# Local attention, token mixing and a gated MLP on one core: channel mixing and output by seven products of quarters, shorter angles, split value loads, constant matmuls, a new order

## The chip, the core and the metric

One core of one Trainium2 chip. The metric is the time of one execution in microseconds (us). TensorE (PE) multiplies matrices, VectorE (DVE), ScalarE (ACT) and GpSimd (POOL) do the elementwise work, SyncE (SP) issues all DMAs. SBUF has 128 partitions; PSUM has 8 banks of 128 x 512 f32, into which PE accumulates.

## What is computed

Two batches, 8 heads, 768 tokens, head width 64, model width 512. The reference, cut to what matters:

```python
# attention: window |i-j| < 16, and 24 summaries of blocks of 32 tokens
k_sum, v_sum = k.max over each block of 32, v.mean over each block of 32
scores = concat(where(window, q @ k.T / 8, -1e9), q @ k_sum.T / 8 + log(32))
a = softmax(scores);  x = a @ concat(v, v_sum)        # heads side by side: (2, 768, 512)
# token mixing by rotation
theta = x @ w_theta                                   # 512 x 512
y = w_tok_r @ (x * cos(theta)) + w_tok_i @ (x * sin(theta))   # 768 x 768 each
u = x + y
x = u + relu(u @ w_ch)                                # channel mixing, 512 x 512
# gated MLP
h = gelu_tanh(x @ w_in);  u, v = halves of h          # 512 x 1024
v = layernorm(v) * g_ln
v = w_sg @ v + b_sg                                   # 768 x 768 over tokens
out = x + (u * v) @ w_out                             # 512 x 512
```

The weights arrive as 64-bit floats; the kernel reads them as bits and puts f32 together itself.

## The kernel before

**Precision.** Every large product is made of three matmuls. Each f32 operand is split into a high part (a copy rounded to fp32r; L324 on ACT, L326 on POOL, L329 on DVE) and a low part (source minus high part, `diff`, L332, on DVE or POOL), and `mm3` (L337 to L339) adds high x high, high x low and low x high into one bank. "A product" below is such a triple.

**Weights.** `unit` (L406) loads 128 rows by one DMA of 512 KB (L414) and makes f32 by one ACT step (L420) and one DVE step (L427); then it splits.

**Attention** works on pairs of heads `p` (`at_pair`: loads of k, q, vT and vW; block maxima L472) and on half pairs `p_hf` (`at_unit`): scores `S` (mask L516, window L523, summaries L530), row maximum `m` (DVE L535), subtraction `d` (L541), exp `e` (ACT L549), transposes `PT` (L554) and their copies `Pt`, values `O` (L568), normalisation `n` (DVE L577, L578, L581), transposes `X` (L590) and copies and splits of x. Pairs 0 to 3 are batch 0; `n3_1` is the last normalisation of batch 0.

**Mixing.** `theta` (twelve row tiles `th0` to `th11`): four products, then on ACT the nearest whole number of turns `kk` (L615) and a correction `kb` (L618), on DVE two steps `ra` (L623) and `rr` (L629, a custom instruction) that bring the angle into reach of the sine; `rotated` makes |angle| (`ab`), cosine and sine on ACT (`sc`, L650, L651) and the products with x (L656). `mixed` adds the products `y` and then x (L693).

**Channel mixing** `ch` (in a batch: 4 output chunks x 2 token ranges of 512 and 256 x 4 products), relu and sum on DVE (L754). **MLP**: `in_v` (gelu L768, layernorm), `in_u` (gelu L799), `sg` (gate L815, product L820), `outp` (4 x 2 x 4 products, sum L833, DMA L836).

**Order.** Nothing schedules at run time. `PLAN`, a table of some 900 words such as `ch0_0_0_0.P.4` (step, engine, place), is played from first to last by `Steps.play` (L247); each engine gets its steps in that order and the places say which part of SBUF or which bank a result takes. A step waits for those it names and for whoever used its place. All DMAs lie on SP's queue in the table's order.

Of the kernel before, what the change touches and what calls it, by code (L numbers as in the profile page):

```python
# [9 lines left out]
F32 = mybir.dt.float32  # L10
# [24 lines left out]
C1 = 6.28125  # L35
C2 = 2.0 * math.pi - 6.28125
PI_LO = 3.1415925
# [6 lines left out]

PLAN = """
k1.S.2712 ones.V masks.G q0_0.S.2688 q1_0.S.168 warm.V.148 fill.P.0 k0.S.100 ks1.V.0 q2_1.S.76
identb.V S1_0.P.0.1 ks0.V.1 m1_0_1.V.2 m1_0_0.V.3 q0_1.S.52 S0_1.P.2.3 vT0.S.4 vT1.S.336 k2.S.288
d1_0_0.V.243 m0_1_1.V.4 m0_1_0.V.3 d1_0_1.V d0_1_0.V.198 d0_1_1.V ks2.V.3 e1_0.A q2_0.S.552
S0_0.P.4.5 m0_0_1.V.4 m0_0_0.V.2 d0_0_0.V.103 S2_0.P.3.2 S2_1.P.1.0 m2_0_0.V.1 d2_0_0.V.507
d0_0_1.V m2_0_1.V.1 d2_0_1.V m2_1_0.V.4 m2_1_1.V.1 e0_1.A e0_0.A e2_0.A vT3.S.459 q1_1.S.435  # L50
S1_1.P.4.6 PT1_0_1.P.5 sets.G m1_1_0.V.0 PT1_0_0.P.3 PT0_0_0.P.7 PT2_0_1.P.2 d2_1_0.V.243 d2_1_1.V
m1_1_1.V.4 d1_1_0.V.55 Pt0_0_0.A.435 d1_1_1.V vs0.G.5 v0_0.S.386 wth0d.S.704 wth0t.A.0 v0_1.S.655
sums.G v1_1.S.606 vp0.P.7 vm0.A.0 v1_0.S.911 vT2.S.863 PT0_0_1.P.1 vs3.G.6 e2_1.A k3.S.815
PT2_0_0.P.7 PT0_1_0.P.0 vs1.G.3 PT2_1_1.P.4 vs2.V.0 vp1.P.6 vr0_0.G wth2d.S.1088 Pt0_0_1.A.552
q3_1.S.582 wth1d.S.1024 q3_0.S.168 v2_0.S.975 e1_1.A vm1.A.1 wr0d.S.1280 v2_1.S.1231 v3_0.S.6
Pt1_0_0.A.124 O0_0_0.P.1 Pt1_0_1.A.100 v3_1.S.1182 wi0d.S.1472 vr0_1.G Pt2_0_1.V.1158 wth3d.S.1408
wri1d.S.1344 wri0d.S.1664 ks3.V.3 wi1d.S.1600 Pt0_1_0.A.435 O0_0_1.P n0_0.V.4.288 wth2t.A.1
PT0_1_1.P.6 vr1_0.G vp2.P.3 vp3.P.2 PT1_1_1.P.5 O1_0_0.P.0 vm3.V.0 PT1_1_0.P.1 wri2d.S.1536
Pt2_0_0.A.552 Pt2_1_1.A.124 Pt0_1_1.V.219 wth1t.A.2 PT2_1_0.P.7 wth0r.V.68 Pt1_1_1.A.195 O0_1_0.P.6
wth0h.G.2688 Pt2_1_0.A.435 k4.S.1872 wr1d.S.1808 O1_0_1.P vm2.V.2 n1_0.V.4 O0_1_1.P wth1r.V.256  # L60
vr2_0.A S3_0.P.3.4 n0_1.V.4.864 vr1_1.G Pt1_1_0.A.100 wth1h.A.1920 S3_1.P.7.0 m3_0_0.V.6 X0_0.P.1
m3_1_1.V.4 wr3d.S.1744 wth0l.G xe0_0.A O1_1_0.P.6 d3_0_0.V.770 X1_0.P.5 wth2r.V.68 m3_0_1.V.6
d3_0_1.V vr2_1.A vr3_0.A O2_0_0.P.1 wr0t.A.1 O2_1_0.P.3 O2_1_1.P xh0_0.G.2064 e3_0.A O1_1_1.P
O2_0_1.P xl0_0.G wr2d.S.2240 th1_0.P.4 m3_1_0.V.3 wr0r.V.224 xe1_0.A PT3_0_1.P.2 X0_1.P.5
wr0h.G.1984 n1_1.V.6 PT3_0_0.P.6 d3_1_0.V.103 xh1_0.A.528 d3_1_1.V xl1_0.G Pt3_0_1.A.195
Pt3_0_0.A.1158 e3_1.A wth1l.V wth2h.G.384 xe0_1.A n2_0.V.4 xh0_1.G.480 th0_0.P.2 wi0t.A.1 th2_0.P.6
vr3_1.A O3_0_0.P.0 O3_0_1.P PT3_1_1.P.1 xl0_1.G vT4.S.2192 X2_0.P.5 n2_1.V.3 q4_0.S.2168 xe2_0.A
PT3_1_0.P.3 th0_1.P X2_1.P.5 n3_0.V.4 Pt3_1_0.V.195 X3_0.P.3 wth2l.G wth3t.A.2 Pt3_1_1.V.1158
xh2_0.G.2064 O3_1_0.P.1 wth3r.V.256 O3_1_1.P xl2_0.G q4_1.S.2144 th3_0.P.0 xe3_0.V th1_1.P
wth3h.A.0 xh3_0.V.144 n3_1.V.4 th2_1.P ks4.V.3 X3_1.P.1 wth3l.G X1_1.P.3 xl3_0.G xe2_1.V th0_2.P  # L70
th0_3.P wri0t.A.2 xe1_1.V wi1t.A.0 th1_2.P wr0l.G xh1_1.A.528 th1_3.P q5_0.S.2120 xe3_1.V th2_2.P
xh3_1.V.96 xl1_1.V kk0.A.192 xh2_1.G.720 kb0.A.224 kk1.A.256 ra0.V.1440 kb1.A.192 v4_0.S.2447
th2_3.P rr0.V ab0_0.V.1408 S4_0.P.2.1 v4_1.S.2398 vs4.V.4 ra1.V.224 vp4.P.3 m4_0_0.V.6 m4_0_1.V.4
wi2d.S.2334 sc0_0.A vT5.S.2640 th4_0.P.4 th3_1.P xl2_1.G d4_0_0.V.2195 xl3_1.G th3_2.P th5_0.P.2
d4_0_1.V th3_3.P th4_1.P zm0_0.G v5_1.S.2591 q6_0.S.2310 vm4.A.0 vr4_0.A kk2.A.256 e4_0.A
wi0r.V.2559 zh0_0.A.464 k5.S.2511 rr1.V wri1t.A.1 PT4_0_0.P.1 wi0h.G.2048 q5_1.S.1128 PT4_0_1.P.3
ra2.V.1504 th4_2.P Pt4_0_0.A.2171 kk3.A.192 O4_0_0.P.1 wri0r.V.1472 wi0l.V zl0_0.G Pt4_0_1.V.2567
vr4_1.G wri0h.G.576 vs5.V.4 O4_0_1.P S4_1.P.3.6 ab1_0.A.2208 wr1t.A.2 vp5.P.5 th4_3.P sc1_0.A
ks5.V.6 n4_0.V.0.768 m4_1_0.V.4 wri0l.G wr1r.V.1408 y0_0_0_0.P.1.7 vm5.A.0 kk4.A.1472 v5_0.S.1079
# [181 lines left out]
def kernel(  # L261
# [648 lines left out]
```

## Time and profile before

| what | us |
|---|---|
| runs of the kernel before | 400.04, 401.49, 402.1 (median 401.49) |
| the profiled execution: its own time | 400.38 |
| its span (first to last instruction) | 398.6 |
| PE busy | 382.7 |
| DVE busy | 243.2 |
| POOL busy | 194.6 |
| ACT busy | 161.2 |

The profiled execution lies 1.1 us below the median, and 1.8 us lie around its span. [...] How long a matmul really holds PE is read from the distance of the starts.

### The profile page before, as it was taken

The page shows a single profiled execution, that of the slowest core. Times are in us where ns is not written, and L with a number is a line of the kernel's source. Part 1 is how long each engine was busy: PE and PEld are TensorE (multiplying, and loading weights), DVE is VectorE, ACT ScalarE, POOL GpSimd, SP SyncE. Part 2 cuts the span into 40 slices and gives each one's busy share as a digit, 9 for nine tenths or more (in the row PEclk, how much of TensorE's full clock was granted, in tenths as well). Part 3 has the DMA queues.
Part 4 walks back from the last instruction along what each step waited for, and adds up shares of the span by engine and source line. Part 5 has one row for each costly group of instructions (what it writes and reads, how often), then busy time and mean ns, then how long its engine had stood idle before and what let it go on. Part 6 is the DMA issues. An engine that isn't in the chain of part 4 may idle for free.

```text
span 398.6 us, 7716 instructions
## 1 busy us (share of the span) xinstructions
PE 382.7 (96%) x3104; PEld 328.3 (82%) x3104; DVE 243.2 (61%) x426; ACT 161.2 (40%) x291; POOL 194.6 (49%) x219
## 2 busy tenths in 40 slices
PE   7787999899999999999999999999999999999996
PEld 4666878688878888888888888888888888889885
DVE  4884899989989676526445836764571444117242
ACT  1385679879898663503321220414260020111000
POOL 6642678477642638317758454730620357417100
PEclk9695999989999999999999999999999999999999
DMA  7999994544164413204303000000011000000134
GB/s 266 303 330 353 346 250 134 157 124 129 37 228 159 132 54 135 104 0 152 140 0 107 1 2 0 0 2 1 2 53 39 2 0 2 0 2 0 41 119 158
DMA packets 17090, 40.49 MB, mean 102 GB/s; under 512 B 2080, under 2 KB 7456, under 8 KB 17056
## 3 DMA queue, kind: packets, MB, share of 16 engines
q1 hardware_dynamic: 17056, 40.01, 31.3%
q8 instruction: 24, 0.39, 0.4%
q14 instruction: 10, 0.08, 0.1%
HBM read 36.86 MB, written 3.15 MB: 100 GB/s over the span
## 4 chain that ended last, share of the span: by engine, by line
PE 81%; DVE 5%; issue 1%; DVEq 0%
PE bank L337 26%; PE bank L338 25%; PE bank L339 25%; PE bank L568 2%; PE bank L554 1%; PE bank L523 1%; DVE small L535 1%; PE bank L590 1%; DVE xT L329 0%; PE bank L530 0%; DVE small L472 0%; DVE page1F L644 0%; DVE page8F L541 0%; PE bank L516 0%; DVE page5F L541 0%
## 5 line engine op out<-in xcount | busy, mean ns | idle before, releaser
L815 DVE SCALAR_TENSOR_TENSOR page5F<-bank,g_sb,page8F 128x256 f32<-128x256 f32 (+1 forms) x11 | 6.6, 602 | 21.4 <-PE bank L339 18.0
L833 DVE TENSOR_TENSOR page5F<-bank,xT 128x512 f32<-128x512 f32 (+1 forms) x15 | 8.1, 564 | 18.2 <-PE bank L339 18.2
L693 DVE TENSOR_TENSOR xT<-bank,xT 128x256 f32<-128x256 f32 (+1 forms) x16 | 8.4, 549 | 17.5 <-PE bank L339 17.5
L535 DVE TENSOR_REDUCE small<-bank 128x3 f32<-128x360 f32 x32 | 16.0, 523 | 4.6 <-PE bank L530 4.6
L754 DVE SCALAR_TENSOR_TENSOR xT<-bank,xT 128x512 f32<-128x512 f32 (+1 forms) x16 | 8.3, 550 | 12.0 <-PE bank L339 12.0
L420 ACT ACTIVATE stage<-page8F 128x512 f16<-128x512 bf16 x8 | 6.1, 785 | 17.8 <-DVE page5F L427 16.8
L820 POOL TENSOR_TENSOR page5F<-page5F,page7F 128x512 f32<-128x512 f32 (+1 forms) x6 | 6.7, 1117 | 12.1 <-ACT page7F L799 12.1
L326 POOL TENSOR_SCALAR page4R<-xT 128x512 fp32r<-128x512 f32 (+1 forms) x4 | 2.4, 601 | 18.8 <-PE bank L339 9.8
L332 POOL TENSOR_TENSOR page6R<-page1F,page6R 128x512 fp32r<-128x512 f32 x2 | 2.6, 1285 | 17.9 <-DVE page6R L329 16.2
L799 ACT ACTIVATE page7F<-bank 128x256 f32<-128x256 f32 (+1 forms) x8 | 3.8, 495 | 15.0 <-PE bank L339 10.0
L324 ACT ACTIVATE page3R<-page5F 128x256 fp32r<-128x256 f32 (+1 forms) x3 | 1.5, 486 | 20.3 <-DVE page5F L820 15.3
L815 DVE SCALAR_TENSOR_TENSOR page7F<-bank,g_sb,page8F 128x512 f32<-128x512 f32 (+1 forms) x4 | 2.4, 610 | 10.4 <-PE bank L339 10.4
L324 ACT ACTIVATE page10R<-xT 128x512 fp32r<-128x512 f32 x2 | 1.3, 632 | 17.1 <-PE bank L339 11.2
L337 PE MATMUL bank<-page10R,page2R 128*128 128x512 f32 x20 | 8.1, 405 | 0.0
L420 ACT ACTIVATE stage<-page5F 128x512 f16<-128x512 bf16 x8 | 6.3, 792 | 4.2 <-DVE page5F L427 2.6
L338 PE MATMUL bank<-page3R,page2R 128*128 128x256 f32 (+1 forms) x26 | 8.0, 308 | 0.0
L339 PE MATMUL bank<-page3R,page2R 128*128 128x256 f32 (+1 forms) x26 | 8.0, 307 | 0.0
L337 PE MATMUL bank<-page3R,page2R 128*128 128x256 f32 (+1 forms) x26 | 7.9, 305 | 0.0
L338 PE MATMUL bank<-page10R,page2R 128*128 128x512 f32 x20 | 7.9, 395 | 0.0
L339 PE MATMUL bank<-page10R,page2R 128*128 128x512 f32 x20 | 7.8, 391 | 0.0
L799 ACT ACTIVATE page8F<-bank 128x512 f32<-128x512 f32 (+1 forms) x3 | 1.6, 526 | 15.4 <-PE bank L339 15.4
L338 PE MATMUL bank<-page4R,page6R 128*128 128x256 f32 (+1 forms) x24 | 7.7, 320 | 0.0
(1029 smaller groups left out, 1572.3 us busy)
## 6 DMA issues: line engine op xcount, KB each, us to landing
out_dram<-page5F SPq DMA_DIRECT2D x8, 256.0 KB, 2.0
page8F<-in_w_out_dram SPq DMA_DIRECT2D x3, 511.8 KB, 3.6
page12F<-in_vW_dram SPq DMA_DIRECT2D x4, 290.2 KB, 7.3
page5F<-in_w_theta_dram SPq DMA_DIRECT2D x2, 511.8 KB, 10.8
page9F<-in_w_rT_dram SPq DMA_DIRECT2D x2, 511.8 KB, 7.2
page11F<-in_w_rT_dram SPq DMA_DIRECT2D x2, 511.8 KB, 5.8
page12F<-in_w_iT_dram SPq DMA_DIRECT2D x2, 511.8 KB, 7.9
page5F<-in_w_iT_dram SPq DMA_DIRECT2D x2, 511.8 KB, 3.9
```

What stands on the lines that cost most here:

```text
L337: PE.matmul(ps, ah, bh, start=first, stop=False, skip_group_check=True)
L338: PE.matmul(ps, ah, bl, start=False, stop=False, skip_group_check=True)
L339: PE.matmul(ps, al, bh, start=False, stop=last, skip_group_check=True)
L420: ACT.activation(T(nm + "s", F16).rearrange("p (n t) -> p n t", t=2)[:, :, 1], raw[:, :, 2], AF.Copy)
L535: op(f"m{u}_{h}", "V", lambda e, h=h: DVE.tensor_reduce(out=T(f"m{u}_{h}"), in_=s3(h), axis=AX.X, op=ALU.max), after=[f"S{u}"], new=[(f"m{ ...
L568: PE.matmul(ps[64 * ab:64 * ab + 64, o:o + 65], sb[:WC, t * P + 64 * ab:t * P + 64 * ab + 64], v[:WC, c:c + 65], start=True, stop=True)
L693: DVE.tensor_tensor(out=dst, in0=ps, in1=dst, op=ALU.add)
L754: DVE.scalar_tensor_tensor(out=dst, in0=T(bk)[:, :n], scalar=0.0, in1=dst, op0=ALU.max, op1=ALU.add)
L799: op(bk + "g", "A", lambda e, half=half, f=f, n=n, bk=bk: ACT.activation(T(f"ut{b}_{half}_{f}"), T(bk)[:, :n], AF.Gelu_apprx_tanh), after= ...
L815: DVE.scalar_tensor_tensor(out=T(gf), in0=T(bk)[:, :n], scalar=g_sb[:, f:f + 1], in1=T("bsg")[:, o:o + n], op0=ALU.mult, op1=ALU.add)
L820: op(f"gm{b}_{half}_{f}", "VG", lambda e, gf=gf, ut=ut: EN[e].tensor_tensor(out=T(gf), in0=T(gf), in1=T(ut), op=ALU.mult), after=[f"ga{b}_ ...
L833: op(bk + "e", "V", lambda e, half=half, c=c, n=n, bk=bk: DVE.tensor_tensor(out=T(bk + "s"), in0=T(bk)[:, :n], in1=xs(b, c, half), op=ALU. ...
```

## The change

1. **Seven products of quarters.** u @ w_ch and gated @ w_out are done by a scheme of seven products of quarters (tokens and channels halved, as Strassen and Winograd have it). Of each operand `sums_of` makes four sums of quarters, and `split` splits quarters and sums. Bank A runs through four terms and is copied out after each of the first three (`snapshot`), banks B and C hold the rest; DVE adds the pieces. `in_u` and `sg` now work on 2 x 384 tokens instead of 512 + 256.
2. **Angles in turns.** w_theta is scaled by 1/(2 pi) when it is split; `kb` and the custom step fall away, one `rr` per tile stays, and the sine is given the scale 2 pi.
3. **Value loads split at row 32**: 16 loads of 96 rows become 32 of 32 and 64 rows.
4. **Constant matmuls.** `keep_busy`: 17 matmuls of 480 columns in groups of 8, 1, 2, 5 and 1 at five places of the attention of batch 0.
5. **A new order**: the whole of `PLAN` is new, the rest follows it. Exp and sine steps are grouped, so that ACT loads its tables 9 times, before 15.

The diff, cut to its core:

```diff
+IDLE = (8, 1, 2, 5, 1,)
 PLAN = """
...
+winv3d.S.2496 winv3t.A.1 ch0_1Ac0.A.1896 u1_0q0l.G u1_0+1.V u1_1+0.V.2352 u1_1q0h.A.1632
+ch1_0A_0_0.P.3 u1_0+2.V.2304 u1_0q2h.A.384 ch1_1A_0_0.P.7 u1_0+3.V u1_1q0l.V u1_1+2.V.1296
...
+    def keep_busy(i, n):
+        def f(e):
+            for j in range(n):
+                PE.matmul(T(f"idle{i}")[:, :5 * WK], identb[:],
+                          maskb[:].rearrange("p m c -> p (m c)"), start=True, stop=True)
+        return f
...
+            for rr in (slice(0, 32), slice(32, WK)):
+                nc.sync.dma_start(T(f"v{p}_{hf}")[rr], vW[b, r, rr, VH * hf:VH * hf + VH])
...
-        op(f"kb{n}", "A", lambda e: ACT.activation(T(f"kb{n}"), T(f"kk{n}", I32), AF.Copy,
-                                                   scale=-C2),
-            DVE._custom_dve(TENSOR_ADD_SAT, out=T(f"rr{n}"), in0=T(f"rr{n}"), in1=T(f"kb{n}"),
-                            s0=PI_LO, s1=-PI_LO)
+        op(f"rr{n}", "V", lambda e: DVE.scalar_tensor_tensor(
+            out=T(f"rr{n}"), in0=T(f"kk{n}", I32), scalar=-1.0, in1=T(f"th{n}"), op0=ALU.mult,
...
+    TERMS = {"A": (("11", "11"), ("S2", "T2"), ("S3", "T3"), ("22", "T4")), "B": (("12", "21"),),
+             "C": (("S1", "T1"), ("S4", "22"))}
+    def sums_of(nm, n, x1, x2, after, use, left):
...
+        for j, (p, q, o) in enumerate(todo):
+            op(f"{nm}+{j}", "VG", lambda e, j=j, p=p, q=q, o=o: EN[e].tensor_tensor(
+                out=s(j)(), in0=p(), in1=q(), op=o), after=after + pre[j], cols=n,
+        split(f"{nm}q0", n, half(x1, 0), after, use)
+        split(f"{nm}q1", 2 * n, x2, after, use)
+        for k in range(2):
+            split(f"{nm}q{2 + k}", 2 * n, lambda k=k: T(f"{nm}s{k}"), [f"{nm}+{2 * k + 1}"],
...
+    def seven(bk, n, pairs, na, nb, ca, cb, flip, snap):
+        for bank, terms in TERMS.items():
+            for j, (l, r) in enumerate(terms):
+                for i, (a, b) in enumerate(pairs):
+                        mm3(T(name)[:, :n], x, y, first, end)
+                if bank == "A" and j < 3:
+                    pre = pre + [snap(j, name, last[bank, j])]
+                elif bank == "C" and j == 0:
+                    pre = pre + [f"{bk}22"]
...
+    QUARTERS = {"11": ("B", 0, 0), "22": ("C", 0, 2), "12": ("C", 1, 1), "21": ("A", 3, None)}
+            last = seven(bk, 384, [(f"wc{d}", f"u{b}_{d}") for d in range(2)], 256, 384,
+                         sl(c), slice(0, 384), False, snapshot(bk, 384))
+                    op(bk + q, "V", lambda e, bk=bk, bank=bank, m=m: DVE.tensor_tensor(
+                        out=T(f"{bk}m{m}"), in0=T(bk + bank)[:, :384], in1=T(f"{bk}m{m}"),
...
+                    DVE.scalar_tensor_tensor(out=dst, in0=src, scalar=0.0, in1=dst,
+                                             op0=ALU.max, op1=ALU.add)
```

`TERMS` gives bank A four terms, B one and C two; with two row blocks (`pairs`) that is 14 products for an output chunk `c`, and 28 in a batch.

**Place 1: SP's queue in the first part.** Names: `kT`, `qT`, `vT`, `vW` are attention's inputs, 128 x 2047 16-bit words are one weight unit; `page4F` and so on are parts of SBUF. The rows before, from the twelfth DMA on:

```order
L467 DMA page2F<-in_vW_dram 96x774
L414 DMA page3F<-in_w_theta_dram 128x2047
L467 DMA page3F<-in_vW_dram 96x774 x2
L467 DMA page4F<-in_vW_dram 96x774
L461 DMA page4F<-in_vT_dram 128x768
L459 DMA page4F<-in_kT_dram 128x768
L414 DMA page5F<-in_w_theta_dram 128x2047
L464 DMA page3F<-in_qT_dram 128x384
L414 DMA page5F<-in_w_theta_dram 128x2047
L464 DMA page0F<-in_qT_dram 128x384
```

And of the change, from its tenth DMA on:

```order
L500 DMA page2F<-in_vT_dram 128x768
L498 DMA page2F<-in_kT_dram 128x768
L503 DMA page1F<-in_qT_dram 128x384
L453 DMA page2F<-in_w_theta_dram 128x2047
L503 DMA page3F<-in_qT_dram 128x384
L500 DMA page3F<-in_vT_dram 128x768
L503 DMA page3F<-in_qT_dram 128x384
L500 DMA page3F<-in_vT_dram 128x768
L453 DMA page4F<-in_w_theta_dram 128x2047
L509 DMA page4F<-in_vW_dram 32x774
L509 DMA page4F<-in_vW_dram 64x774
```

The fourth k (page4F before, page2F now) and the q behind it have moved ahead of two weight units and of all value loads: what stands ahead of and in the load of that k is 5896 KB before and 3264 KB now. The last value load of batch 0 has moved the other way, from 8976 KB to 10384 KB.

**Place 2: PE at the start of channel mixing.** Before, every product adds to a bank that nobody reads until its last (the first matmul of each product; L338 and L339 follow it):

```order
L337 MATMUL bank_67<-page3R,page6R 128x512
L337 MATMUL bank_69<-page4R,page6R 128x256
L337 MATMUL bank_66<-page4R,page6R 128x256
L337 MATMUL bank_64<-page12R,page0R 128x512
L337 MATMUL bank_67<-page12R,page6R 128x512
```

Now, likewise (L353 and L354 follow each), with the last matmul of bank A's first term at the top:

```order
L354 MATMUL bank_69<-page8R 128x384
L352 MATMUL bank_63<-page3R,page11R 128x384
L352 MATMUL bank_66<-page3R 128x384
L352 MATMUL bank_70<-page3R 128x384
L352 MATMUL bank_68<-page3R,page11R 128x384
L352 MATMUL bank_69<-page3R,page11R 128x384
```

Bank 69 is bank A of the second chunk of batch 0. Between the end of its first term and the start of its second, when the bank must have been copied out, stand four products for other banks.

**Place 3: DVE in the same stretch, of the change.**

```order
L344 COPY page9F<-bank_67 128x384
L742 TENSOR_TENSOR xT<-bank_70,xT 128x512
L813 TENSOR_TENSOR page9F<-xT,page9F 128x384
L813 TENSOR_TENSOR page12F<-xT 128x384 x2
L813 TENSOR_TENSOR page12F<-xT,page9F 128x384
L347 TENSOR_TENSOR page8R<-xT,page8R 128x384
L813 TENSOR_TENSOR page6F<-xT 128x384
```

The first row is a copy of a bank A, the second a sum for `u`; the five behind it are sums of quarters and a low part, both of whose sources lie in SBUF. None of the L813 rows has a counterpart before.

## Rows read from the trace of the kernel before

**Rows 1.** The page's busy times by engine, and PE in 40 slices.
```profile
PE 382.7 (96%) x3104; PEld 328.3 (82%) x3104; DVE 243.2 (61%) x426; ACT 161.2 (40%) x291; POOL 194.6 (49%) x219
PE   7787999899999999999999999999999999999996
```
**Rows 2.** Windows: stretch, its us, then busy us (instructions) by engine, PEclk, DMA share, GB/s.
```profile
0.00:50.20 50.20, 41.06 (x706) 33.35 (x707) 35.15 (x81) 24.66 (x42) 28.00 (x58) 0.83 0.99 319
50.20:101.70 51.50, 48.20 (x724) 40.65 (x723) 48.58 (x89) 42.73 (x72) 36.47 (x35) 0.97 0.54 152
101.70:395.40 293.70, 293.45 (x1679) 254.27 (x1677) 159.00 (x258) 93.86 (x179) 130.17 (x128) 1.00 0.16 55
395.40:398.60 3.20, 0.00 (x0) 0.00 (x0) 0.42 (x1) 0.00 (x0) 0.00 (x0) 1.00 0.39 140
```
**Rows 3.** The same for ten microseconds of the first stretch.
```profile
30.00:40.00 10.00, 7.82 (x135) 6.99 (x136) 4.76 (x10) 5.09 (x9) 2.85 (x4) 0.54 1.03 354
```
**Rows 4.** Timeline of PE there: start, us, instructions, idle before and its releaser.
```profile
28.48 0.39 PE L530 MATMUL bank<-small,page0F 64*64 64x24 f32 x13
32.18 0.52 PE L530 MATMUL bank<-small,page0F 64*64 64x24 f32 x10 [3.31 <-issue]
```
**Rows 5.** The same view of DVE, at the first of its maxima and at the end of batch 0's attention.
```profile
32.67 0.53 DVE L535 TENSOR_REDUCE small<-bank 128x3 f32<-128x360 f32 x1 [2.17 <-PE bank L530]
...
49.66 0.56 DVE L581 TENSOR_TENSOR page4F<-bank,small 128x384 f32<-128x384 f32 x1
```
**Rows 6.** Timeline of SP's queue: when three loads were issued.
```profile
5.79 0.52 SPq L461 DMA_DIRECT2D page2F<-in_vT_dram  x1
...
12.61 0.64 SPq L459 DMA_DIRECT2D page4F<-in_kT_dram  x1
...
27.21 0.35 SPq L414 DMA_DIRECT2D page7F<-in_w_theta_dram  x1
```
**Rows 7.** DMAs by source: count, KB each, us from issue to landing; the same three loads.
```profile
page7F<-in_w_theta_dram SPq DMA_DIRECT2D x1, 511.8 KB, 9.9
...
page2F<-in_vT_dram SPq DMA_DIRECT2D x1, 384.0 KB, 6.8
...
page4F<-in_kT_dram SPq DMA_DIRECT2D x1, 384.0 KB, 10.7
```
**Rows 8.** Timeline of PE in the third stretch: three products, and the next start.
```profile
290.69 0.28 PE L337 MATMUL bank<-page2R,page0R 128*128 128x256 f32 x1
...
291.04 0.40 PE L337 MATMUL bank<-page13R,page0R 128*128 128x512 f32 x1
...
292.42 0.28 PE L337 MATMUL bank<-page2R,page0R 128*128 128x256 f32 x1
```
**Rows 9.** Windows again: all engines, then L332 alone (DVE, POOL), from channel mixing on.
```profile
214.20:395.40 181.20, 181.18 (x996) 157.66 (x995) 89.34 (x153) 36.85 (x64) 69.64 (x69) 1.00 0.06 21
...
214.20:395.40 181.20, 30.86 (x35) 43.54 (x35) 1.00 0.06 21
```
**Rows 10.** Groups by form: count, busy us, mean ns, idle before. DVE, and a copy on ACT.
```profile
L332 DVE TENSOR_TENSOR page4R<-page5F,page4R 128x512 fp32r<-128x512 f32 x3 | 2.0, 680 | 0.0
L332 DVE TENSOR_TENSOR page4R<-page1F,page4R 128x512 fp32r<-128x512 f32 x1 | 1.8, 1803 | 0.0
L693 DVE TENSOR_TENSOR xT<-bank,xT 128x512 f32<-128x512 f32 x8 | 5.4, 681 | 3.1 <-PE bank L339 3.1
L693 DVE TENSOR_TENSOR xT<-bank,xT 128x256 f32<-128x256 f32 x8 | 3.3, 418 | 14.5 <-PE bank L339 14.5
L324 ACT ACTIVATE xT<-bank 128x384 f32<-128x384 f32 x8 | 3.9, 486 | 7.0 <-PE bank L590 6.9
```
**Rows 11.** Windows of the angle steps: L629 on DVE, then L618 on ACT.
```profile
0.00:214.20 214.20, 10.14 (x12) 0.95 0.53 169
...
0.00:214.20 214.20, 7.38 (x12) 0.95 0.53 169
```
**Rows 12.** Timeline of DVE: the last sum before the last output DMA.
```profile
395.42 0.42 DVE L833 TENSOR_TENSOR page5F<-bank,xT 128x256 f32<-128x256 f32 x1 [0.29 <-PE bank L339]
```

More of the change, by code (lines that the diff above doesn't have):

```diff
@@ L50 @@
[L50 to L55, printed above, removed]
@@ L394, with high, low @@
     op("fill", "P", filler, after=["warm"], use=["warm"], new=[("warmb", "B", 1)])
-    def high_low(nm, src, after):
+    def keep_busy(i, n):
[4 more added lines that the diff above has]
+        return f
+    for i, n in enumerate(IDLE):
+        op(f"idle{i}", "P", keep_busy(i, n), after=["identb"], new=[(f"idle{i}", "B", 1)])
+    def high_low(nm, src, after):
+        if nm.startswith("wth"):
+            def high(e):
+                if e == "A":
+                    ACT.activation(T(nm)[:, :512], T(src), AF.Copy, scale=INV2PI)
+                else:
+                    POOL.tensor_scalar(out=T(nm)[:, :512], in0=T(src), scalar1=INV2PI,
+                                       scalar2=0.0, op0=ALU.mult, op1=ALU.add)
+            def low(e):
+                DVE.scalar_tensor_tensor(out=T(nm)[:, 512:], in0=T(src), scalar=INV2PI,
+                                         in1=T(nm)[:, :512].bitcast(F32), op0=ALU.mult,
+                                         op1=ALU.subtract)
+            op(nm + "h", "AG", high, after=[after], use=[src], new=[(nm, "R", 4096)])
+            op(nm + "l", "V", low, after=[nm + "h"], use=[src, nm])
+            return
         op(nm + "h", "AG", lambda e: copy(e, T(nm)[:, :512], T(src)), after=[after], use=[src],
@@ new lines, in snapshot, with snap @@
+    def snapshot(bk, n, scale=None):
+        def snap(j, name, after):
+            g = scale[1 if j == 2 else 0] if scale else None
+            op(f"{name}c{j}", "A" if scale else "AV",
+               lambda e: ACT.activation(T(f"{bk}m{j}"), T(name)[:, :n], AF.Copy,
+                                        scale=g) if scale
+               else copy(e, T(f"{bk}m{j}"), T(name)[:, :n]),
+               after=[after] + ["gsb"] * bool(scale), use=[name], new=[(f"{bk}m{j}", "F", 4 * n)],
+               cols=n)
+            return f"{name}c{j}"
+        return snap
@@ new lines, in gate @@
+                def gate(e, f=f, bk=bk, gf=gf, s=s):
+                    DVE.scalar_tensor_tensor(
+                        out=T(gf)[:, s], in0=T(bk)[:, :384], scalar=g_sb[:, f:f + 1],
+                        in1=T("bsg")[:, s], op0=ALU.mult, op1=ALU.add)
+                op(f"ga{b}_{th}_{f}", "V", gate, cols=384,
+                   after=[last, "gsb", "bsg"] + [f"ga{b}_0_{f}"] * th,
+                   use=[bk, "bsg"] + [gf] * th, new=[] if th else [(gf, "F", 4 * S)])
+                op(f"gm{b}_{th}_{f}", "VG", lambda e, gf=gf, s=s, ut=ut: EN[e].tensor_tensor(
+                    out=T(gf)[:, s], in0=T(gf)[:, s], in1=T(ut), op=ALU.mult),
+                   after=[f"ga{b}_{th}_{f}", ut + "g"], use=[gf, ut], cols=384)
```

612 lines of the change are left out of this document (344 added, 268 removed).

## The prediction

> **What bounds the kernel now.** First the busy times: PE 382.7 of 398.6 us, no other engine above 243 [rows 1]. Then the windows, to see where the rest lies [rows 2]. From 101.7 us to 395.4 PE is busy for 293.45 of 293.70 us at full clock, and the others for half of it: there PE's list of work alone sets the time, and every matmul saved is worth its length. Ahead of that, in two stretches of 50.2 and 51.5 us, PE has 9.1 and 3.3 us of idle time, a granted clock of 0.83 and 0.97, and DVE is as busy as PE or nearly so (48.58 of 51.50 in the second). In the first stretch the DMA engines are full (share 0.99) until batch 0's attention is done. So the kernel has a first part bound by loads and by chains over DVE, a second bound by DVE and PE together, and a long third bound by PE.
>
> The timeline shows the largest single loss: PE stops within one step, the scores of unit `3_0`, for 3.31 us, and was released by nothing that the profile shows ("issue") [rows 4]; DVE's maxima wait for it, 2.17 us in the first row [rows 5], and in 30 to 40 us the clock is 0.54 and DVE has only 4.76 us of work [rows 3]. [...]
>
> For the third stretch I need PE's true pace. Starts of products lie 0.35 us apart for three matmuls of 256 columns and 1.38 for six of 512 (290.69, 291.04, 292.42) [rows 8]: 0.117 and 0.230 us for one.
>
> **The sum, stretch by stretch**, against the profiled execution, 400.38 us.
>
> *Third stretch, products.* Channel mixing and output have 96 matmuls of 512 and 96 of 256 columns each, for both batches: 96 x (0.230 + 0.117) = 33.3 us, twice that 66.6. The change has 168 of 384 columns each. No row shows 384. Its bounds are the price of 256 (0.117, which no matmul of more columns should beat: −27.3) and of 512 (0.230: +10.7). The two rows give 0.457 and 0.449 ns a column, one price to within 2%, so a step up to 0.230 between them is excluded and 0.18 is the most I keep (+2.2). I take the middle, 0.173: 336 x 0.173 = 58.3, a gain of **8.3 us**, an eighth. `in_u` and `sg` at 2 x 384 instead of 512 + 256 cost the same by this price.
>
> *Third stretch, moved.* Counted in the two orders at these paces, PE has 2.9 us less of attention, theta and y products left when `th6_0` begins (before: at 101.7 us), because four units' transposes and values and two theta products have moved ahead. They are paid in the second stretch.
>
> *Third stretch, added around PE.* Each chunk copies bank A three times: 2 stages x 2 batches x 2 chunks x 3 = 24 copies, 16 on ACT and 8 on DVE, 0.49 us each by the nearest row (128x384 from a bank, on ACT) [rows 10]. In the order at least three other products stand between the end of a term and the next matmul of its bank (place 2 has four, 4 x 3 x 0.173 = 2.1 us), and the copy, its start and its signal need less than that if the engine is free. If the cover were gone, each would cost about 0.65 us. From the last y product of batch 1 on (214.2 us before) DVE's list grows from 83 to 124 us at undisturbed lengths: 20 of the 48 sums of quarters (POOL does the others), and sums and copies of 384 columns, which I price between the rows of 256 and 512 (0.42 and 0.68) at 0.55 [rows 10], and low parts of 768 columns at 0.97, in the same way. POOL's grows from 65 to 86, ACT's from 37 to 65. PE's is 176. DVE as a whole still fits, but not evenly: counted in pieces of 10 us of PE's list, DVE has 12.9 and 13.4 us in the two in which batch 0's channel mixing runs, and 15.3 in one near the first `in_u`. Taken as a backlog this is 5.4 us after the first two and 8.8 at its highest; the two pieces ahead have only 2.6 and 7.1 us of DVE work. I charge **3 us** of late waits, with bounds of 0 (the pieces ahead take the excess) and 9 (the backlog is waited for in full). Third stretch: 293.7 − 8.3 − 2.9 + 3.0 = **285.5**, bounds 282.5 and 293.7 (9 of waits, 0.18).
>
> *Second stretch.* Two angle steps per tile go, 10.14/12 = 0.85 us on DVE and 7.38/12 = 0.62 on ACT [rows 11]; six of the twelve tiles lie here: −5.1 on DVE and −3.7 on ACT. Against that stand three units' `d`, two `m`, a normalisation and the copies of P that moved in. By the lists DVE goes from 49.1 to 47.3, PE from 45.2 to 47.7, ACT from 38.3 to 43.7 less its table loads. DVE is 94% busy there now [rows 2], so a list 1.8 shorter gives some, and PE's 2.5 more takes it back: **51.5**, unchanged; bounds 49.5 (DVE's ratio kept) and 54 (PE's addition all shows).
>
> *First stretch.* A load that was issued at 12.61 landed 10.7 us later (23.3); the load that ended where the fourth k now ends was issued at 5.79 and took 6.8 (12.6) [rows 6, 7]. So scores of `3_0` can begin up to 10.7 us earlier, on SP's queue the value loads pay for it (place 1). They end at 10,384 KB; a load that ended at 10,000 KB landed at 27.21 + 9.9 = 37.1, so the last lands near 38.5, and with its two values steps and the normalisation [rows 5] the attention of batch 0 can't end before 41. That the value loads are two DMAs now adds 8 issues of 0.35 to 0.64 us [rows 6] in this part; I cost them at nothing, since the DMA engines behind that queue are full, and at 8 x 0.5 = 4 us if they weren't. DVE's list to that point is 4.0 us shorter (four copies of P go to ACT, others to POOL). 41 is one end; 50.2 the other, if the 3.3 us stop comes again with its low clock at another place and DVE's idle time isn't what ends. I take the middle, **45.5**. The 17 constant matmuls cost 17 x 0.230 x 480/512 = 3.7 us at the full clock [rows 8], or twice that, 7.3, at the lower; PE's 9.1 idle us of this stretch hide them, and they stand ahead of steps that wait for ACT or for loads. Without that cover they would cost just that.
>
> *End.* The last sum works on 384 columns instead of 256 (0.55 for 0.42 [rows 12]) and its DMA is 192 KB instead of 128: 3.2 becomes **3.5**, bounds 3.2 and 4.
>
> 45.5 + 51.5 + 285.5 + 3.5 + 1.8 around the span = 387.8. The profiled execution lies 1.1 below the median of the runs shown, and I add that: **389 us**.
>
> [...] The low parts on DVE with both sources in SBUF take 680 ns, and one of the same form took 1803; sums with one source in a bank keep to 681 [rows 10]. [...]
>
> **Rivals.**
>
> 1. *The start doesn't get shorter.* The stop, or a late load, moves along with the order, and the constant matmuls cost what they hide or don't hold the clock: then the fourth part of the change does nothing. For it: the DMA share is 0.99 all through the stretch, and the bytes ahead of the last value load grow. Against it: 3.6 us of PE's stop and DVE's wait have no cause in the order of the steps. The first stretch stays at 50.2: 393.7. Chance 0.18.
> 2. *Copies of bank A and sums of quarters come late.* DVE's two excesses show in full, or the copies are exposed at 0.65 us in half of the 24 cases (7.8): 9 instead of 3 us of late waits, **395**. For it: the two dense pieces; against it: from channel mixing on DVE was busy for 89 of 181 us [rows 9], so much of this can be done ahead of its use. Chance 0.13.
> 3. *Slower: DVE becomes the bound from channel mixing on.* Of its 203 steps there 95 have two SBUF sources (51 before), and POOL's list grows too. At undisturbed lengths (0.68 for 512 columns, 0.42 for 256) the 35 low parts of that stretch should take 21.4 us; they took 30.86 [rows 9], 0.27 more each. If each of the 95 is stretched by s, DVE needs 124.4 + 95 s, with 176 for PE: it takes over at s = 0.54, and the gain of 12.6 is gone at s = 0.70. If all were blocked as in the worst row (1.1 more) it would need 229, some 53 us beyond PE: 440. At the 0.27 seen it needs 150; twice 0.27, with POOL a third busier, is the point from which it decides. Chance 0.07; from 402 on.
>
> **The numbers.** Forecast 0.62, rivals 0.18, 0.13 and 0.07. Low end: 41 + 49.5 + 282.5 + 3.2 + 1.8 + 1.1 = 379. High end: the first two rivals together are 399.7; 398 leaves out the third rival and the worst of that pair. So 379 to 398. A measurement of this kernel tells a difference of about 0.5% (2 us) from none. Faster by more than that needs less than 399.5: the forecast and both of the first rivals, less the cases in which they come together: 0.90. Within it 0.03, slower 0.07.
>
> **What would show it.** The last normalisation of batch 0 ends near 45 us; no PE wait named "issue" of 3 us ahead of it; a clock above 0.83 there. Starts of matmuls of 384 columns lie 0.17 us apart. From theta of the seventh tile on PE is idle for about 3 us, in waits for the copies or for sums of quarters. DVE's two-source rows of 384 columns at 0.55 to 0.9. It is wrong if PE waits for DVE or POOL for over 9 us behind 100 us, if 384 columns cost over 0.19, or if the first stretch is not shorter.

## The result and the profile after

| | median us (lowest to highest) | ratio to before, 95% interval |
|---|---|---|
| before | 400.76 (397.89 to 402.1) | |
| changed | 386.62 (383.3 to 386.88) | 0.9637 [0.9561, 0.9713] |
| changed, run again on another occasion | 385.68 (383.19 to 387.59) | 0.9624 [0.9577, 0.967] |

The kernel is 14 us faster; 389 was forecast, with 379 to 398 as the range. The profiled execution took 386.78 us, 384.9 of it span. Cut at the same points as before (the end of batch 0's last normalisation, the start of `th6_0`, the last product), its windows are:

```profile
0.00:45.90 45.90, 38.60 (x720) 30.37 (x721) 32.43 (x73) 23.26 (x46) 28.08 (x61) 0.89 0.93 319
45.90:96.70 50.80, 50.21 (x765) 42.21 (x764) 46.84 (x87) 40.98 (x76) 37.81 (x37) 1.00 0.50 164
96.70:380.20 283.50, 282.68 (x1593) 260.71 (x1591) 202.12 (x308) 107.17 (x201) 154.04 (x131) 1.00 0.17 59
380.20:384.90 4.70, 0.02 (x1) 0.00 (x0) 0.56 (x1) 0.00 (x0) 0.00 (x0) 0.85 0.48 181
```

Columns as in [rows 2], which they answer to. The four stretches took 50.2, 51.5, 293.7 and 3.2 us; they take 45.9, 50.8, 283.5 and 4.7. PE now idles for 7.3 us in the first and 1.4 in the next two together.

The pace of 384 columns, which no row of before had, in the timeline of PE in the third stretch:

```profile
288.75 0.33 PE L352 MATMUL bank<-page7R,page5R 128*128 128x384 f32 x1
...
291.35 0.33 PE L352 MATMUL bank<-page13R,page3R 128*128 128x384 f32 x1
```

The second row is the fifteenth start after the first: 2.60/15 = 0.173 us. What PE waited for in the whole run (us in total, times, longest):

```profile
PE bank L565 <- issue: 2.4, 1, 2.4
PE bank L558 <- DVE identb L390: 2.0, 1, 2.0
PE bank L408 <- DVE page14F L367: 1.7, 1, 1.7
PE bank L627 <- issue: 1.2, 1, 1.2
...
PE bank L353 <- DVE page8R L347: 0.4, 1, 0.4
PE bank L352 <- DVE page6F L344: 0.4, 1, 0.4
```

The last two are all that the whole seven-product scheme, its copies and its sums make PE wait. The two stops by "issue" are of the kind of [rows 4]. From channel mixing on, all engines and then the low parts alone (L347; DVE, POOL), against [rows 9]:

```profile
203.30:380.20 176.90, 176.07 (x961) 168.27 (x959) 135.37 (x210) 58.87 (x100) 88.84 (x76) 1.00 0.12 39
...
203.30:380.20 176.90, 37.05 (x40) 49.04 (x34) 1.00 0.12 39
```

DVE is busy for 135 of 177 us there, before for 89 of 181. And the end, in the timeline of DVE, which answers to [rows 12]:

```profile
380.25 0.56 DVE L1006 TENSOR_TENSOR page6F<-bank,page6F 128x384 f32<-128x384 f32 x1 [0.42 <-PE bank L354]
```

and in that of SP's queue:

```profile
379.60 0.40 SPq L1011 DMA_DIRECT2D out_dram<-page1F  x1
380.09 1.27 SPq L1011 DMA_DIRECT2D out_dram<-page6F  x2
```

The last sum ends at 380.81, and 4.1 us follow; before it was 395.84 and 2.7 us. Three outputs of 192 KB are issued from 379.60 on.

### The profile page after: what moved, and what is told of

Its sections match the earlier page's. It is cut to its first block, busy times and chain, and to the rows that moved or that the text cites. A ratio compares the mean times of both kernels' runs of the same rounds, so it can differ in the third digit from the quotient of the medians.

```text
span 384.9 us, 7757 instructions
## 1 busy us (share of the span) xinstructions
PE 371.5 (97%) x3073; PEld 333.3 (87%) x3073; DVE 281.9 (73%) x468; ACT 171.4 (45%) x321; POOL 219.9 (57%) x227
## 4 chain that ended last, share of the span: by engine, by line
PE 88%; DVE 6%; issue 2%; ACT 2%; DMA 1%; SPq 0%; DVEq 0%; ACTq 0%
PE bank L352 25%; PE bank L353 25%; PE bank L354 24%; PE bank L627 3%; PE bank L613 3%; PE bank L565 2%; PE bank L649 1%; PE bank L414 1%; PE bank L572 1%; DMA page0F<-in_kT_dram 1%; DVE xT L899 1%; DVE page8R L347 1%; PE bank L558 1%; DVE page7R L347 1%; DVE page12F L813 0%
## 5 line engine op out<-in xcount | busy, mean ns | idle before, releaser
L742 DVE TENSOR_TENSOR xT<-bank,xT 128x512 f32<-128x512 f32 (+1 forms) x16 | 8.3, 547 | 6.5 <-PE bank L354 6.5
L347 POOL TENSOR_TENSOR page3R<-xT,page3R 128x384 fp32r<-128x384 f32 x6 | 6.8, 1128 | 8.3 <-ACT page3R L339 5.7
L347 POOL TENSOR_TENSOR page2R<-xT,page2R 128x384 fp32r<-128x384 f32 x7 | 7.1, 1025 | 6.5 <-ACT page2R L339 4.2
L973 DVE SCALAR_TENSOR_TENSOR page1F<-bank,g_sb,page10F 128x384 f32<-128x384 f32 x8 | 4.7, 613 | 8.3 <-PE bank L354 8.3
L339 ACT ACTIVATE page10R<-page4F 128x512 fp32r<-128x512 f32 (+1 forms) x2 | 1.5, 740 | 20.0 <-PE bank L353 19.9
L979 POOL TENSOR_TENSOR page1F<-page1F,page6F 128x384 f32<-128x384 f32 x6 | 6.6, 1113 | 5.9 <-DVE page1F L973 4.7
L347 POOL TENSOR_TENSOR page2R<-page9F,page2R 128x512 fp32r<-128x512 f32 x6 | 8.7, 1446 | 1.7 <-ACT page2R L339 1.5
L347 POOL TENSOR_TENSOR page1R<-page9F,page1R 128x512 fp32r<-128x512 f32 x2 | 4.6, 2312 | 7.2 <-ACT page1R L339 7.2
L352 PE MATMUL bank<-page0R,page2R 128*128 128x512 f32 (+1 forms) x21 | 8.5, 405 | 0.0
L347 POOL TENSOR_TENSOR page8R<-page10F,page8R 128x512 fp32r<-128x512 f32 (+1 forms) x3 | 4.6, 1522 | 6.3 <-ACT page8R L339 6.3
L354 PE MATMUL bank<-page0R,page2R 128*128 128x512 f32 (+1 forms) x21 | 7.8, 373 | 0.0
L353 PE MATMUL bank<-page0R,page2R 128*128 128x512 f32 (+1 forms) x21 | 7.8, 371 | 0.0
L558 PE MATMUL bank<-maskb,identb 64*64 64x288 bf16 x64 | 5.2, 315 | 2.0 <-DVE identb L390 2.0
L339 ACT ACTIVATE xT<-bank 128x384 f32<-128x384 f32 x11 | 5.2, 490 | 3.8 <-PE bank L649 3.8
L347 POOL TENSOR_TENSOR page3R<-page4F,page3R 128x512 fp32r<-128x512 f32 x2 | 2.6, 1308 | 7.1 <-ACT page3R L339 7.1
L459 ACT ACTIVATE stage<-page11F 128x512 f16<-128x512 bf16 x8 | 6.2, 786 | 0.9 <-DVE page7F L466 0.9
```

The lines of the kernel that those rows point to most:

```text
L339: ACT.activation(dst, src, AF.Copy)
L347: EN[e].tensor_tensor(out=lo, in0=src, in1=hi.bitcast(F32), op=ALU.subtract)
L352: PE.matmul(ps, ah, bh, start=first, stop=False, skip_group_check=True)
L353: PE.matmul(ps, ah, bl, start=False, stop=False, skip_group_check=True)
L354: PE.matmul(ps, al, bh, start=False, stop=last, skip_group_check=True)
L558: PE.matmul(s3(h)[sl(ab, 64), :, :WK], identb[rr, rr], maskb[rr, m:m + 3], start=True, stop=False, skip_group_check=True)
```

## The experiments

Theory: the products give their eighth in the third stretch; the start gains by its order, held up by loads, stops and a low clock. Rivals: copies or sums come late; the start's other parts do nothing. Below, "attention ends" stands for the end of batch 0's last normalisation and "th6" for the start of `th6_0`, each in the run's own profiled execution.

**The changed kernel again.**

> The changed kernel unchanged, as the measure for the three that follow on the same chip. All theories: 383 to 387 us, a ratio of 0.96 to 0.97, PE idle for about 1 us from 100 us to its end.

385.68 us. Attention ends at 45.59, th6 is at 96.44. The milestone behind th6 keeps its distance in both profiles of this kernel (last product 283.5 us later). What differs from execution to execution lies ahead of that, in the start.

**Without the constant matmuls.**

```diff
-IDLE = (8, 1, 2, 5, 1,)
+IDLE = ()
-... idle0.P.3 PT0_0_0.P.4 m1_0_0.V.1 idle1.P.3 PT0_1_0.P.1 e1_1.A
+... PT0_0_0.P.4 m1_0_0.V.1 PT0_1_0.P.1 e1_1.A
```

> The changed kernel without its 17 constant matmuls. Theory (they fill PE's idle time and hold the granted clock): the clock between 15 and 35 us falls below the 0.92 of 20 to 30 us that the changed kernel shows, matmuls behind them run at the lower level, and the time grows by 2 to 4 us. Rival (they only fill time that PE has to wait in anyway): within 1 us of the changed kernel. Second rival (they delay the steps behind them): 1 to 3 us faster.

382.05 us (381.57 to 384.47), 0.9552 [0.9512, 0.9592] of before: 3.6 us faster than the changed kernel on the same chip, and the fastest of all runs. The two intervals still overlap by a little, but five of its six executions are faster than all ten of the changed kernel. In the traces attention ends at 42.13 instead of 45.59, and from there on all distances are the same (th6 at 92.99). The second rival held, if with more than its 3 us, and the clock did not fall. Windows of 10 to 20 us, of the changed kernel:

```profile
10.00:20.00 10.00, 7.59 (x168) 5.62 (x161) 8.73 (x19) 2.41 (x3) 7.06 (x14) 0.67 1.04 366
```

and without the constant matmuls:

```profile
10.00:20.00 10.00, 7.37 (x247) 6.63 (x242) 9.29 (x19) 5.56 (x11) 8.30 (x16) 1.00 1.04 366
```

PE does 247 matmuls instead of 168 there, at full clock. In the changed kernel's timeline the first group alone takes

```profile
17.07 3.38 PE L414 MATMUL bank<-maskb,identb 128*128 128x480 bf16 x8
```

at half the clock (0.50 from 17.07 to 20.45 us, the lowest that any window here gives; "the lower level" below is this one), with the first transposes of P behind it. That isn't the price of the matmuls alone. The run with copies done twice (below) keeps all 17 and differs only from channel mixing on. In its trace the clock was full again from 11.6 us on, the same group took

```profile
15.29 1.79 PE L414 MATMUL bank<-maskb,identb 128*128 128x480 bf16 x8
```

and attention ended at 42.89. The ends of attention in the timelines of DVE, of the changed kernel again, without constant matmuls, and with copies twice (start and length):

```profile
45.04 0.56 DVE L640 TENSOR_TENSOR page4F<-bank,small 128x384 f32<-128x384 f32 x1
41.57 0.56 DVE L640 TENSOR_TENSOR page4F<-bank,small 128x384 f32<-128x384 f32 x1
42.33 0.56 DVE L640 TENSOR_TENSOR page4F<-bank,small 128x384 f32<-128x384 f32 x1
```

So at full clock the 17 delay the start by 0.8 us; the other 2.7 us of the first pair go with the lower clock, which came behind the first stop in both profiles of the changed kernel and not in the other two, and with longer stops than in the run with copies twice. Whether the constant matmuls bring that about is open.

**The constant matmuls in the kernel before.** The same five groups, put into the old table ahead of the same steps.

> The kernel before with the 17 constant matmuls at the places where the change has them (8 before the first transposes of P, 1, 2, 5 before the scores of 3_0, 1 before the values of 3_1). Theory (they hold the clock): the clock of 10 to 20 us rises above 0.68, and the time falls by 1 to 3 us. Rival (PE has no idle time at these places in the old order, and they delay what follows): 1 to 4 us slower.

402.17 us, 1.0029 [1.0001, 1.0057]: slower by 1.4, hardly clear of none. Attention ended at 52.4 instead of 50.2, but most of that delay is older than the constant matmuls. From 21.4 us to 41.8 the granted clock was full, as the theory had it (0.54 before in 30 to 40 us). The 1.00 that the view also gives for 10 to 20 us is not a measurement: the clock records of this trace begin only at 21.37, and a window without records reads as 1.00. The rows show the lower level there. Here are the same 24 window scores, and what PE does next once the scores of the first six units are done, first in the timeline of PE of this run, then of the kernel before:

```profile
11.54 1.21 PE L530 MATMUL bank<-page0F,page14F 64*64 64x96 f32 x24
20.86 2.02 PE L400 MATMUL bank<-maskb,identb 128*128 128x480 bf16 x8
```

```profile
9.22 0.70 PE L523 MATMUL bank<-page0F,page14F 64*64 64x96 f32 x24
17.89 1.53 PE L554 MATMUL bank<-ident,page1F 128*120 128x128 f32 x6
```

PE was 3.0 us late when the first constant matmul began, and 2.2 late at the end of attention. What the 17 matmuls cost or gave in the old order stays open. (The 0.83 of [rows 2] and the 0.89 of the changed kernel's first stretch are upper bounds for the same reason: their records begin at 6.87 and 4.57 us.)

**Value loads whole again, and split in the kernel before.**

```diff
-                for rr in (slice(0, 32), slice(32, WK)):
+                for rr in (slice(0, WK),):
```

> The changed kernel with its value loads whole again, 96 rows in one DMA, 16 instead of 32. Theory (the split is worth nothing: the DMA engines are full there): within 1 us of the changed kernel, the last normalisation of batch 0 ends at 45 to 47 us. Rival (the parts land earlier): it ends 2 us later and the time grows by 1 to 2 us.

> The kernel before with its value loads split at row 32. Theory (worth nothing): within 1 us of the kernel before. Rival (the parts land earlier): 1 to 2 us faster.

Whole: 387.38 us, 0.9676 [0.9637, 0.9716], 1.7 slower, an interval that overlaps that of the changed kernel; attention ends at 46.67. Split in the old order: 396.51 us, 0.9883 [0.9839, 0.9927], 4.2 faster; attention ends at 48.53 (in an execution of 398.78 us, its slowest). The rival held in the second, by more than it said; the first alone doesn't decide. The DMA view of the changed kernel (us from issue to landing last):

```profile
page6F<-in_vW_dram SPq DMA_DIRECT2D x4, 193.5 KB, 4.3
...
page5F<-in_vW_dram SPq DMA_DIRECT2D x2, 193.5 KB, 4.2
page6F<-in_vW_dram SPq DMA_DIRECT2D x4, 96.8 KB, 4.2
```

and with the loads whole:

```profile
page6F<-in_vW_dram SPq DMA_DIRECT2D x4, 290.2 KB, 11.0
...
page5F<-in_vW_dram SPq DMA_DIRECT2D x2, 290.2 KB, 9.1
```

The time from issue to landing falls to half in these rows, but that doesn't make a transfer twice as fast. In every trace here at most eight DMAs of this queue are under way at once, and eight halves hold about half the bytes: 2.6 to 2.9 MB were under way when these whole loads were issued, 1.2 to 1.8 MB with these split ones of batch 0. Other split loads of batch 0, issued with 2.1 to 2.5 MB under way, took 6.3 to 9.1 us. What counts is when the loads land. The last value load of batch 0 landed at 34.7 us in the kernel before and at 32.6 split; at 37.8 with the loads whole in the new order, at 36.4 and 37.7 in the two profiles of the changed kernel. In the first 40 us the DMA engines moved 316 GB/s at a share of 0.98 with the loads whole and 315 at 0.92 in the changed kernel, so with loads of 96 rows they were busy a little longer for the same bytes. Why was not tried.

**One angle step for two, in the kernel before.**

```diff
-        op(f"kb{n}", "A", ...
-            DVE._custom_dve(TENSOR_ADD_SAT, ...
+        op(f"rr{n}", "V", lambda e: DVE.scalar_tensor_tensor(
+            out=T(f"rr{n}"), in0=T(f"th{n}"), scalar=INV2PI, in1=T(f"kk{n}", I32), op0=ALU.mult,
+            op1=ALU.subtract), ...
```

> The kernel before, in its order, with one angle step on DVE in place of two and one on ACT in place of two (the scale by 1/(2 pi) is applied to theta in that step instead of to w_theta). DVE loses 10.1 us and ACT 7.4, six of the twelve tiles in the second stretch, where DVE is 94% busy. Theory (DVE's list sets the second stretch): 3 to 5 us faster, theta of the seventh tile begins at 97 to 99 us instead of 101.7. Rival (the stretch is set by waits between the engines): less than 1 us faster.

397.24 us, 0.9905 [0.9877, 0.9933]: 3.5 faster. Its attention ended later in this profile (52.1), but the second stretch took 48.1 us instead of 51.5. The theory held in size. ACT lost steps there too, and the run doesn't part them: that DVE's list sets this stretch rests on its busy share [rows 2].

**Both of these parts in the old order.**

> The kernel before with two parts of the change, in its own order: one angle step on DVE for two (and one on ACT for two), and value loads split at row 32. Alone they were worth 3.5 and 4.2 us. Theory (they act in different stretches, the loads ahead of the end of batch 0's attention, the angle steps behind it): they add to 6 to 8 us, 393 to 395 us, and of the changed kernel's gain without constant matmuls (18 us) that leaves 10 to 12 for the products and the order. Rival (the stretch in front hides what the other gives): 4 to 5 us, 396.

393.32 us, 0.9805 [0.9769, 0.9842], against 401.04 on that chip: 7.7 faster, the sum of 3.5 and 4.2. They act in different stretches: attention ends at 46.89, 3.3 us earlier than before, and from there to the last product it takes 341.5 us instead of 345.2.

**Every copy of bank A twice.**

```diff
...
-               else copy(e, T(f"{bk}m{j}"), T(name)[:, :n]),
+               lambda e: [copy(e, T(f"{bk}m{j}"), T(name)[:, :n]) for _ in range(2)],
```

> The changed kernel with each of the 24 copies of bank A done twice, 0.49 us more on ACT (16) or 0.55 on DVE (8) each time, between a term's end and the bank's next matmul. Theory (the copies are covered by the products that stand between): less than 2 us slower, PE's idle time from 200 us to its end stays below 3 us. Rival (they lie on PE's path): 24 x 0.5 = 12 us slower, in waits of PE for the line of the copies.

388.36 us, 2.7 slower. From th6 to the last product 287.3 instead of 283.5: of the 12 us of copies added 3.8 show, PE's idle time in that stretch going from 0.8 to 3.2. (The median shows less than that: the start of this kernel varies, and the profiled execution is its fastest.) It is a little more than the theory allowed and far from the rival's 12. The cover is real and nearly used up: one copy is hidden, the second in part.

**More instructions ahead of the stop.** The kernel before:

```diff
-        for j in range(8):
-            PE.matmul(ps, warm[:, :P], warm[:, P:640], start=True, stop=True)
+        for j in range(32):
+            PE.matmul(ps[:, :P], warm[:, :P], warm[:, P:2 * P], start=True, stop=True)
```

> The kernel before with its 8 opening matmuls of 512 columns made into 32 of 128: 24 more matmuls, each with a weight load, 48 more instructions on PE for the same columns. PE stopped for 3.31 us at its 961st record of the trace, with no releaser. Theory (the stop is PE running out of instructions, whose next block comes too late among full DMA engines): it moves 24 matmuls ahead in the program, out of the summary scores (L530) of unit 3_0 into its window scores (L523), and the number of the instruction at which it stops stays within a few. Rival (the step itself waits for something that the profile does not name): the stop stays in L530. The time in either case within 2 us of the kernel before.

402.77 us, 1.0053 [1.0023, 1.0084], 2.0 slower. The stop moved as the theory said, in the timeline of PE, with [rows 4] to compare:

```profile
32.25 0.49 PE L523 MATMUL bank<-page4F,page0F 64*64 64x96 f32 x13
35.58 0.46 PE L523 MATMUL bank<-page4F,page0F 64*64 64x96 f32 x10 [2.84 <-issue]
```

It is the window scores of `3_0` now, again after thirteen, 24 matmuls earlier. Counting PE's records in each trace (matmuls, weight loads and the sequencer's few waits, by start) all stops that nothing released stand at a multiple of 256 apart:

| kernel | record at the stop: idle us |
|---|---|
| before | 450: 0.90; 961: 3.31 |
| changed | 450: 2.41; 1218: 1.21 |
| without constant matmuls | 450: 2.29; 705: 0.76; 961: 1.22; 1218: 1.31 |
| before, more instructions | 450: 1.39; 705: 2.88; 961: 2.84; 1218: 1.88 |

450, 705, 961 and 1218 are 194 + 256 k, within one. In the traces of all other runs that have such stops they stand at the same records too (one at 1217). The pages of the two kernels list a queue `q8 instruction: 24, 0.39`: 24 packets in 0.39 MB, where PE has 6208 matmuls and weight loads before and 6146 now, 259 and 256 to a packet. That fits blocks of 256 instructions of PE; whose instructions a packet holds the page doesn't say. The stops show only early: behind 1218, where PE's matmuls are long, no trace has such a stop of over 0.3 us, while ahead of it PE's steps are many and short and the DMA share is 0.8 to 1.0 in windows of 10 us. That full DMA engines bring the stops about was not tried by itself.

**Fewer instructions.** Masks of a scores step by two matmuls on the whole array instead of four on quarters; then also summaries by 6 f32 matmuls of 128 rows for 12 of 64. The first alone and both in the changed kernel without constant matmuls, both in the kernel before.

```diff
-                    PE.matmul(s3(h)[sl(ab, 64), :, :WK], identb[rr, rr], maskb[rr, m:m + 3],
+                PE.matmul(s3(h)[:, :, :WK], identb[:], maskb[:, hf:hf + 3],
...
-                        PE.matmul(s3(h)[sl(ab, 64), t, WK:], q[rr, sl(2 * t + ab, 64)],
-                                  ks[rr, :], start=False, stop=True, skip_group_check=True)
+                    PE.matmul(s3(h)[:, t, WK:], q[rr, sl(t)], ks[rr, :], start=False, stop=True,
```

> The changed kernel without its constant matmuls, and with the masks of each scores step added by two matmuls on the whole array instead of four on quarters of it: 4 fewer instructions a unit (a matmul and a weight load count as two), 32 fewer ahead of the last normalisation of batch 0, for about the same time on PE. Theory (the start is bound by the supply of instructions, 256 at a time, which in the run without constant matmuls came 5.6 to 6.8 us apart): that normalisation ends 0.7 to 0.9 us earlier than at 42.1, and the time falls by as much. Rival (only PE's own work counts): within 0.5 us of the run without constant matmuls, 382.

> As the run with masks in two, and the scores of the summaries by 6 f32 matmuls of 128 rows in place of 12 of 64: 24 fewer instructions a unit more, 224 fewer in all ahead of the last normalisation of batch 0. Theory (supply of instructions): 7/8 of a block, 4.9 to 6.0 us, if nothing else is late; the last value loads land near 38.5, so 2 to 4 us are to be had at the start, and the time comes to 378 to 380. Rival (PE's own work): a summary step of 0.48 us becomes at best a half, 0.1 to 0.2 us a unit on the path, 1 to 2 us in the start and as much behind it; stops without a releaser as long as before.

> The kernel before with the same two edits, 28 fewer instructions on PE a unit. Theory (supply of instructions): stops without a releaser again at instructions that are multiples of 256 apart, later in the program, and the attention of batch 0 ends 2 to 5 us earlier than at 50.2; the time 396 to 399. Rival (PE's own work): less than 2 us.

Masks alone: 383.57 us, 0.9586 [0.9559, 0.9612]; attention ends at 42.01, hardly earlier than the 42.13 without the edit. Stops fell from 5.6 us to 2.8, but the expectation's "about the same time on PE" was wrong, so this run doesn't tell the theories apart. Both: 395.43 us, 12 slower than masks alone on the same chip; in the kernel before 404.95, 4 to 5 slower. Both theories missed. The stops are gone altogether in both traces, in which PE is slower in the start, for two reasons. The first is the price of the matmuls at full clock. In the timeline of PE of the kernel before with both edits:

```profile
35.41 0.42 PE L515 MATMUL bank<-maskb,identb 128*128 128x288 bf16 x2
35.76 0.72 PE L522 MATMUL bank<-page4F,page0F 64*64 64x96 f32 x24
36.41 0.85 PE L528 MATMUL bank<-small,page0F 64*128 64x24 f32 x12
37.20 0.42 PE L515 MATMUL bank<-maskb,identb 128*128 128x288 bf16 x2
```

and of the same steps in the changed kernel:

```profile
26.25 0.32 PE L558 MATMUL bank<-maskb,identb 64*64 64x288 bf16 x4
26.39 0.67 PE L565 MATMUL bank<-page2F,page3F 64*64 64x96 f32 x24
26.89 0.48 PE L572 MATMUL bank<-small,page3F 64*64 64x24 f32 x24
27.21 0.30 PE L558 MATMUL bank<-maskb,identb 64*64 64x288 bf16 x4
```

By their starts two whole masks take 0.35 us and four quarter ones 0.14; twelve summaries of 64x128 take 0.79 and 24 of 64x64 0.32. The group of eight above, 480 columns each in 1.79 us at full clock, gives an estimate of 0.13 us for 288 columns on the whole array. A whole mask took 0.175, one after the other; four quarter ones of the same 288 columns took 0.14 together, about the time of one, so these ran beside each other: fewer instructions cost more here, 0.68 us a unit.

The second is the clock. With both edits the changed kernel was granted the lower level from 7.8 to 31.7 us (0.50 in the last row of this document). In the kernel before with both edits the clock records begin only at 31.04, and the rows ahead of that show the lower level, for the steps just shown at full clock:

```profile
18.78 0.66 PE L515 MATMUL bank<-maskb,identb 128*128 128x288 bf16 x2
19.37 1.24 PE L522 MATMUL bank<-page1F,page0F 64*64 64x96 f32 x24
20.54 1.48 PE L528 MATMUL bank<-small,page0F 64*128 64x24 f32 x12
```

Of the 12 us that the summaries cost the changed kernel, the two traces have 8.7 ahead of the end of attention (50.67 for 42.01), of which 8 x 0.47 = 3.8 are their price at full clock and the rest goes along with the lower clock. Another 3.6 lie behind it, where batch 1 has eight more units at full clock. Why PE stayed at the lower level there was not tried. So neither run shows what a stop costs. With the masks alone 8 x 0.21 = 1.7 us were added, 2.8 of stops went and 0.1 was gained: how much a stop costs stays open.

## Why the prediction was right

**Products: right.** 0.173 a matmul was the middle between two rows and is what was measured. The third stretch was to be 285.5 and is 283.5.

**Late waits: mis-sized.** The step "I charge 3 us" was too much: PE idles for 0.8 us there. The backlog of DVE that was counted in pieces of 10 us of the order did not hold PE up, presumably because the pieces around them took it; such a list doesn't say when a result is needed. Rival 2 fell with it, as the copies done twice show; the one wait of PE for a copy took 0.4 us, where the prediction put 0.65 on an exposed one.

**DVE beside POOL: right.** The 69 sums, gates and low parts on DVE that have both sources in SBUF took 62.5 us from channel mixing on, 45.2 at their undisturbed lengths by form (0.42, 0.55, 0.68, 0.95): 0.25 us more each, against 0.27 forecast from [rows 9]. s stayed far from 0.54, and rival 3 didn't come. Of the 56 sums and low parts among them (L813, L347), 29 ran while POOL had no work, at 0.95 to 1.02 of these lengths; of the 27 beside work of POOL 8 kept to theirs as well and 19 took 1.3 to 3.8 times as long, up to 2.1 us, as 1.80 in [rows 10]. The mean decides.

**Second stretch: right in size.** 50.8 for 51.5. Two things met there as said: 3.5 us less by the angle steps (as measured in the old order), and products that moved in.

**First stretch: right in size, by wrong steps.** 45.9 for 45.5, the middle between two bounds. "Scores of `3_0` can begin up to 10.7 us earlier" did not happen: they began at 26.25, before at 27.69, since PE's own order ahead of them and not k's load decided. The stop came again, as the other bound supposed, as 2.41 and 1.21 us at other steps. "I cost them at nothing" for the split loads was wrong: alone in the old order they give 4.2 us, and undone in the new one they cost 1.7, which is not clear of noise. "PE's 9.1 idle us of this stretch hide them" for the constant matmuls was wrong too: without them the kernel is 3.6 us faster, of which the traces give 0.8 to their delay at full clock. ("Or twice that, 7.3, at the lower" agrees with the runs: the first group took 3.38 us at 0.50 and 1.79 at 1.00.) Idle time in a stretch was no cover here for a matmul that stands ahead of a step which is already due. The two misses went opposite ways, so that the total came out is in part luck. Of rival 1 the part on the constant matmuls came true, and the start got shorter all the same.

**End: mis-sized.** 4.7 for 3.5, beyond its bound of 4: three outputs of 192 KB are finished within 2 us there and four are issued from 379 us on, and the sum had counted only the last. The DMA share of this stretch is 0.48 for 0.39 before. But before, three outputs of 512 KB together were finished as close to the end, and that the outputs hold each other up was not tried by itself.

**Where the 14.8 us went** (400.52 to 385.68 on one chip): angles −3.5 and split loads −4.2 (measured together −7.7 in the old order), products −8.3 (336 matmuls, from rows), constant matmuls +3.6. This leaves about −2.4 for the new order, less the late waits and the longer end. That rest wasn't measured by itself, no run has the products without the new order, and the split is worth only 1.7 in the new order, so its size stays open. The version to keep is the changed kernel without its constant matmuls.

## What to carry to other kernels

Price a matmul by the distance of starts in the stretch where PE is full; an eighth of the columns was an eighth of the time. Where PE waits, a filler can delay the step behind it as soon as that is due (17 matmuls by 0.8 us here, at full clock): measure the start with and without it. Read a clock of 1.00 against the lengths of the rows (the same 24 scores took 1.21 and 0.70 us), and the time of a DMA from issue to landing against the bytes under way ahead of it (11.0 us for a whole load and 4.3 for a split one, at 2.6 to 2.9 and 1.2 to 1.8 MB). Before counting instructions away, look at which of them run beside each other (four quarter masks in 0.14 us, two whole ones in 0.35).

## What was not expected of the hardware

PE stopped at records a multiple of 256 apart, for up to 3.7 us each (the longest, 3.71, with angles and split loads in the old order), in a stretch with short matmuls and a DMA share of 0.8 to 1.0. Split in two, the last four value loads of batch 0 landed 1.1 to 2.1 us earlier in the old order. The clock was not expected either: with both edits on masks and summaries the changed kernel had 0.50, the lower level, for a window in which PE was busy without a break (the row below). The run without constant matmuls and without these edits had full clock in the same window, with a PE busy for 7.37 of 10 us.

```profile
10.00:20.00 10.00, 10.00 (x118) 7.40 (x116) 6.53 (x13) 2.41 (x3) 8.43 (x17) 0.50 1.04 367
```

Of these two windows the busier one has the lower clock, so how much PE looks busy doesn't tell by itself which clock it is granted.
